# Top-k attention with a maxout layer on one core: small GpSimd steps moved to ScalarE, the k-th score chosen on VectorE, and the order planned anew

## The chip, the cores and the metric

The kernel runs on one core of one Trainium2 chip. The time is the device time of one execution in microseconds (us). The engines are TensorE (PE; its weight loads are listed apart as PEld), VectorE (DVE), ScalarE (ACT), GpSimd (POOL) and SyncE (SP), which here only issues DMAs. Each engine runs its own queue strictly in order and waits for the others by semaphores.

## The reference

Attention over 8 batches, 8 heads, 576 positions and 64 channels keeps for each query the 32 largest scores only; its output, 4608 tokens of 512 channels, goes through a layer that takes the maximum of three products, and an output product.

```python
scores = scale * np.matmul(q, k.transpose(0, 1, 3, 2))
kth = np.partition(scores, -top_k, axis=-1)[..., -top_k:-top_k + 1]
scores = np.where(scores >= kth, scores, -1000000000.0)
attn = np.exp(scores - np.max(scores, axis=-1, keepdims=True))
attn = attn / (np.sum(attn, axis=-1, keepdims=True) + 1e-09)
x = np.matmul(attn, v)            # heads side by side: 4608 x 512
h = np.maximum(np.maximum(x @ w1, x @ w2), x @ w3)
return h @ w_out
```

## The kernel before

The work on attention is cut into 80 units: 64 of four score tiles (nt = 4) and 16 of two (nt = 2), 288 tiles of 128 x 576 scores in all. Every unit passes these steps, named as in the code:

- `qk` (L514) multiplies on TensorE, `evac` (L523) copies the scores to SBUF on ScalarE.
- `sweep` (L532) takes the 8 largest of each stretch of 72 scores on VectorE. `negate` (L538) copies the 4 largest of each stretch with the sign turned, into the tile nA, on GpSimd. `pivot` (L546 to L563, VectorE) finds from both a first bound for the 32nd largest score; its fourth step writes z (L561).
- `sign` (L571, ScalarE) compares a tile with the bound and counts (cnt), `window` (L576, GpSimd) multiplies the scores with that sign, `below` (L580, VectorE) takes the 8 largest of the product. So nine candidates stand in Q.
- `place` (L588, L590, GpSimd) turns the count into a mask over the nine candidates (oh), `pick` (L596, L597, VectorE) multiplies it with Q and takes the maximum: the k-th score.
- `mask` (L620, VectorE) takes out what is smaller, `expo` (L629, ScalarE) makes exponentials and their sums.
- `denominator` (L637, GpSimd) adds 1e-9 to the sums (den), `inverse` (L644, VectorE) takes the reciprocal (rs), `widen` (L649, GpSimd) spreads it over 128 x 128 (rsw).
- `turn` (L675 to L680, TensorE) transposes exponentials and rsw, `turned` (L688, ScalarE) copies them out, `values` (L705, TensorE) multiplies with v, `scaled_x`, `high_x`, `low_x` (L722, L725, L729) scale the result and split it into two 16-bit parts.

The weights come in as 64-bit floats; `decode` (L238 to L240, three VectorE instructions) makes 32-bit ones of them in the first part of the run, and `cut` (L297 to L305) splits these. The feed-forward layers of a batch (`mlp`: products L761, maxima L768 and L770, split L773 and L776, output product L821) fill TensorE's gaps once the batch's attention is done; those of the last batch stand at the end.

The order of every engine's queue is made ahead of time, in Python, by `in_order` (L65 to L129). Every step is a `Piece` with an engine, an assumed cost in ns, the pieces that it needs and a rank: the place of its unit plus a number of the table OFFSETS (L38) for its kind. In a virtual time the planner takes for each engine the first piece by rank that could start within PATIENCE (L136) of the earliest; NEAR (L30) and LATE are assumed latencies between pieces, LEAD (L34) says how far ahead of the lowest rank a piece may be. TensorE takes a feed-forward piece where one can start earlier than attention's (L109 to L114). A piece marked `alone` starts, in this virtual time, only where GpSimd's last piece is about to end, and holds back GpSimd's next:

```python
        if x.alone:
            t = max(t, free["POOL"] + LOCK_A)
        elif x.engine == "POOL":
            t = max(t, shut[0] + LOCK_B)
```

In the kernel before, masks and the pivot's fourth step are marked so. On the chip only the order of each queue is left of the plan, and the semaphores.

Of the kernel before, what the change touches and what calls it, by code (L numbers as in the profile page):

```python
# [22 lines left out]
NW = 9  # L23
# [112 lines left out]
PATIENCE = {'PE': 45.0, 'DVE': 184.0, 'ACT': 29.0, 'POOL': 158.0, 'SP': 0.0}  # L136
# [1014 lines left out]
```

## Time and profile before

| | |
|---|---|
| three runs, us | 1317.75, 1319.06, 1319.50 (median 1319.06) |
| the profiled execution, us | 1317.94 |
| its span, us | 1315.6 |
| busy in the span: PE, DVE, ACT, POOL, us | 1179.5, 1188.1, 1069.0, 848.9 |
| granted TensorE clock, mean share of full speed | 0.98 |

The span runs from the first instruction of the profiled execution to its last; the execution's time has 2.3 us more around it. "Busy" is the time in which at least one instruction of an engine, or of a group of its instructions, was under way, waiting within the instruction included. A group is a line of the code, an engine, an operation and its tiles as out<-in, with the number of instructions behind the x.

### The profile page before, as it was taken

How to read it: one execution, taken by the hardware profiler on the slowest of the kernel's cores; microseconds unless marked ns; L12 is line 12 of the kernel's file. 1: busy time of each engine (PE TensorE's matmuls, PEld its weight loads, DVE VectorE, ACT ScalarE, POOL GpSimd, SP SyncE). 2: the span in 40 equal slices, each digit the busy share in tenths (PEclk: the TensorE clock that was granted, in tenths of full speed). 3: DMA queues.
4: the chain of work that ended last, by engine and by line, in shares of the span. 5: the costliest groups of instructions: out<-in, count | busy, mean ns of one | idle time of the engine just before them, and what ended most of it. 6: DMA issues, size and time to landing. Idle time of an engine off the chain costs nothing. (4 is left out here: it accounts for less than half of the span.)

```text
span 1315.6 us, 30962 instructions
## 1 busy us (share of the span) xinstructions
PE 1179.5 (90%) x9949; PEld 862.7 (66%) x9949; DVE 1188.1 (90%) x5656; ACT 1069.0 (81%) x2544; POOL 848.9 (65%) x1153
## 2 busy tenths in 40 slices
PE   4535897899799999999999999999999999999997
PEld 3323574666586676866676776767767676777775
DVE  7999998999999999999999999999999999997211
ACT  5778887999888989988898989899879998987221
POOL 4468588676677677776777586767676776755110
PEclk9999798999799999999999999999999999999999
DMA  6531110111111101111111011101111101000000
GB/s 184 175 105 36 49 37 25 39 37 37 38 27 36 35 22 52 29 44 25 31 46 27 27 38 44 37 27 28 38 35 29 45 19 35 10 17 1 17 17 28
DMA packets 107018, 53.59 MB, mean 41 GB/s; under 512 B 91744, under 2 KB 99936, under 8 KB 106848
## 3 DMA queue, kind: packets, MB, share of 16 engines
q1 hardware_dynamic: 106848, 51.54, 14.2%
q8 instruction: 80, 1.31, 0.4%
q14 instruction: 90, 0.74, 0.2%
HBM read 42.07 MB, written 9.44 MB: 39 GB/s over the span
## 5 line engine op out<-in xcount | busy, mean ns | idle before, releaser
L576 POOL TENSOR_TENSOR w<-ssb,w 128x576 f32<-128x576 f32 x288 | 423.8, 1479 | 67.9 <-ACT w L571 61.5
L761 PE MATMUL m<-xh,wall 128*128 128x256 f16 (+2 forms) x2448 | 437.0, 279 | 7.0 <-DVE h L770 5.7
L761 PEld LDWEIGHTS <-wall 128*128 128x128 f16 x3672 | 343.5, 98 | 87.5 <-issue 16.0
L761 PE MATMUL m<-xl,wall 128*128 128x256 f16 (+2 forms) x1224 | 335.3, 279 | 0.0
L532 DVE MAX8 L<-ssb 128x8 f32<-128x72 f32 x2304 | 331.3, 216 | 0.0
L620 DVE SCALAR_TENSOR_TENSOR ssb<-ssb,kth 128x576 f32<-128x576 f32 x288 | 262.1, 934 | 2.3
L629 ACT ACTIVATE pm<-ssb,nb 128x576 f32<-128x576 f32 x288 | 223.9, 779 | 43.7 <-DVE ssb L620 41.6
L571 ACT ACTIVATE w<-ssb,Q 128x576 f32<-128x576 f32 x288 | 224.0, 778 | 16.0 <-DVE Q L563 14.7
L688 ACT COPY pT<-tr 128x512 f32<-128x512 f32 (+1 forms) x432 | 216.4, 515 | 24.0 <-PE tr L677 12.2
L680 PE MATMUL tr<-ident,pm 128*128 128x128 f32 x1152 | 184.9, 288 | 48.8 <-ACT pm L629 15.0
L580 DVE MAX8 Q<-w 128x8 f32<-128x576 f32 x288 | 214.1, 748 | 6.4 <-POOL w L576 5.6
L514 PE MATMUL s<-kT,qT 64*128 64x288 f32 x1920 | 181.8, 326 | 20.7 <-ACT ssb L523 11.1
L680 PEld LDWEIGHTS tr<-ident,pm 128*128 128x128 f32 x1152 | 134.3, 145 | 99.4 <-ACT pm L629 31.0
L523 ACT COPY ssb<-s 128x576 f32<-128x576 f32 x288 | 182.1, 644 | 3.9 <-PE s L514 3.3
L514 PEld LDWEIGHTS s<-kT,qT 64*128 64x128 f32 x1920 | 143.1, 199 | 57.4 <-issue 21.3
L705 PE MATMUL tr<-pT,vt 128*64 128x256 f32 (+1 forms) x1920 | 180.3, 339 | 0.5 <-ACT pT L688 0.5
L770 DVE SCALAR_TENSOR_TENSOR h<-m,rises,h 128x256 f32<-128x256 f32 (+2 forms) x204 | 99.7, 489 | 75.5 <-PE m L761 72.5
L776 POOL TENSOR_TENSOR hl<-h,hh 128x256 f16<-128x256 f32 (+2 forms) x102 | 78.9, 774 | 112.3 <-ACT hh L773 111.1
L705 PEld LDWEIGHTS tr<-pT,vt 128*64 128x64 f32 x1920 | 109.4, 141 | 58.0 <-issue 13.3
L821 PE MATMUL m<-wall,hh 128*128 128x512 f16 x432 | 128.7, 379 | 2.6 <-POOL wall L305 1.7
L773 ACT CAST hh<-h 128x256 f16<-128x256 f32 (+2 forms) x102 | 42.5, 417 | 62.1 <-DVE h L770 61.7
L729 POOL TENSOR_TENSOR xl<-xs,xh 128x256 f16<-128x256 f32 (+1 forms) x80 | 56.9, 712 | 44.7 <-ACT xh L725 42.3
(110 smaller groups left out, 1540.8 us busy)
## 6 DMA issues: line engine op xcount, KB each, us to landing
wall<-in_moe_w_dram SPq DMA_DIRECT2D x12, 768.0 KB, 4.7
qt<-in_q_dram SPq DMA_DIRECT2D x68, 128.0 KB, 2.8
kt<-in_k_dram SPq DMA_DIRECT2D x68, 128.0 KB, 2.9
out_dram<-ob SPq DMA_DIRECT2D x32, 256.0 KB, 2.3
vt<-in_v_dram SPq DMA_DIRECT2D x32, 128.0 KB, 2.1
vt<-in_v_dram SPq DMA_DIRECT2D x32, 64.0 KB, 2.2
vt<-in_v_dram SPq DMA_DIRECT2D x96, 16.0 KB, 2.1
vt<-in_v_dram SPq DMA_DIRECT2D x32, 48.0 KB, 2.1
```

The lines of the kernel that those rows point to most:

```text
L514: nc.tensor.matmul(s[:, h, :HALF], qT[sl, qa, c0:c0 + P], kT[sl, ka, i * HALF:(i + 1) * HALF], start=(n_ == 0), stop=(n_ == len(runs) - 1))
L523: nc.scalar.copy(d["both", g][:, :, i * HALF:(i + 1) * HALF], d["s"].pop((g, i))[:, :, :HALF])
L532: nc.vector.max(d["L"][:, t, k, :], d["ssb"][t][:, k * GW:(k + 1) * GW])
L571: nc.scalar.activation(d["w"][t], d["ssb"][t], AF.Sign, bias=d["Q"][:, t, 0:1], scale=-1.0, accum_out=d["cnt"][:, t:t + 1])
L576: nc.gpsimd.tensor_tensor(d["w"][t], d["ssb"][t], d["w"][t], ALU.mult)
L580: nc.vector.max(d["Q"][:, t, 1:NW], d["w"].pop(t))
L620: nc.vector.scalar_tensor_tensor(ss, ss, d["kth"][:, t:t + 1], ss, ALU.is_lt, ALU.subtract, accum_out=d["lost"][:, t:t + 1])
L629: nc.scalar.activation(d["pm", t // 2][:, t % 2], d["ssb"][t], AF.Exp, bias=d["nb"][:, t:t + 1], scale=-1.0 / SHRINK, accum_out=d["sums"][ ...
L680: nc.tensor.transpose(pt[:, j * P:(j + 1) * P], pm[:, i, 64 * i + j * P:64 * i + (j + 1) * P], ident)
L688: nc.scalar.copy(pT[:, 512 * i:512 * i + m] if i < 2 else pT[:, 8 * P:10 * P], pt[:, :m])
L705: nc.tensor.matmul(to, vt[:, block if i < 4 else 8 + h, :], keys, start=(i == 0), stop=(i == 4))
L761: nc.tensor.matmul(box["ps", i][:, :c1 - c0], a, bb[:, kc, c0:c1], start=(kc == 0 and k == 0), stop=(kc == KC - 1 and k == 2))
```

## The change

Four things change.

1. `negate`, `denominator` and `widen` are issued on ScalarE instead of GpSimd.
2. `place` is gone. `pick` has three steps on VectorE: positions compared with the count (L591 of the new file), the product with Q (L594), the maximum (L596). The comparison gives the same 0 or 1 as the difference cut to between 0 and 1.
3. The first two steps of the choice, the weights' decoding and the review at a batch's end are marked `alone`, as masks were.
4. The planner's numbers: assumed costs of a dozen pieces, NEAR, AHEAD_OF_FILL, LEAD, PATIENCE, and all of the 84 OFFSETS. So the order of every queue is another one.

From the choice on, a line has a number lower by one in the new file (mask L619, exponentials L628, den L636, reciprocal L643, rsw L648, x L721, feed-forward product L760, maximum L769, output product L820).

```diff
-NEAR = 60.0
+NEAR = 110.0
...
-AHEAD_OF_FILL = 5
+AHEAD_OF_FILL = 3
...
-LEAD = 20.8
+LEAD = 43.3
...
-PATIENCE = {'PE': 45.0, 'DVE': 184.0, 'ACT': 29.0, 'POOL': 158.0, 'SP': 0.0}
+PATIENCE = {'PE': 2.0, 'DVE': 159.0, 'ACT': 47.0, 'POOL': 7.0, 'SP': 0.0}
...
-                    x = piece("DVE", 1870 if i < 3 else 2500, lambda j=j, j0=j0: decode(j, j0),
-                              [loads[j], *([decoded[j - 1]] if j else []), *([x] if j0 else [])], rank, [("ob", rel), ("ob", rel)])
+                    x = piece("DVE", 1600 if i < 3 else 1950, lambda j=j, j0=j0: decode(j, j0),
+                              [loads[j], *([decoded[j - 1]] if j else []), *([x] if j0 else [])], rank, [("ob", rel), ("ob", rel)], alone=True)
...
-        nc.gpsimd.tensor_scalar(nA[:, :d["nt"]], d["L"][:, :d["nt"], :, 0:4], -1.0, 1.0 / SHRINK, ALU.mult, ALU.mult)
+        nc.scalar.activation(nA[:, :d["nt"]], d["L"][:, :d["nt"], :, 0:4], AF.Copy, scale=-1.0 / SHRINK)
...
-        nc.gpsimd.tensor_tensor(oh[:, :nt], spots.unsqueeze(1).to_broadcast((P, nt, NW)),
-                                d["cnt"][:, :nt].unsqueeze(2).to_broadcast((P, nt, NW)), ALU.subtract)
-        nc.gpsimd.tensor_scalar(oh[:, :nt], oh[:, :nt], 1.0, 0.0, ALU.min, ALU.max)
...
+        if step == 0:
+            nc.vector.scalar_tensor_tensor(best[:, :nt], spots.unsqueeze(1).to_broadcast((P, nt, NW)), 1.0,
+                                           d["cnt"][:, :nt].unsqueeze(2).to_broadcast((P, nt, NW)), ALU.mult, ALU.is_gt)
+        elif step == 1:
+            nc.vector.tensor_tensor(best[:, :nt], best[:, :nt], d["Q"], ALU.mult)
+        else:
+            nc.vector.tensor_reduce(d["kth"], best[:, :nt], AX.X, ALU.max)
...
-        nc.gpsimd.tensor_scalar(d["den"][:, ts], d["sums"][:, ts], 1e-9, 1.0, ALU.add, ALU.mult)
+        nc.scalar.activation(d["den"][:, ts], d["sums"][:, ts], AF.Copy, bias=1e-9)
...
-        nc.gpsimd.tensor_scalar(rsw, d["rs"][:, 2 * g:2 * g + 2].unsqueeze(2).to_broadcast((P, 2, D)), 1.0, 1.0, ALU.mult, ALU.mult)
+        nc.scalar.copy(rsw, d["rs"][:, 2 * g:2 * g + 2].unsqueeze(2).to_broadcast((P, 2, D)))
...
-        p("i", "POOL", 380 + 44 * nt, lambda: place(n), needs=signs, takes=[("oh", held(n, "oh"))])
-        p("h", "DVE", 130 + 20 * nt, lambda: pick(n), needs=[d["i"], *ks])
-        held(n, "oh").append(d["h"])
+        for j in range(3):
+            p(("h", j), "DVE", 60 + 9 * nt, lambda j=j: pick(n, j), needs=[d["h", j - 1]] if j else [*signs, *ks],
+              takes=[] if j else [("oh", held(n, "oh"))], alone=j < 2)
+        held(n, "oh").append(d["h", 2])
...
-        x = piece("DVE", 1170, go, last, (rank, "R"), [("junk", rel)])
+        x = piece("DVE", 1016, go, last, (rank, "R"), [("junk", rel)], alone=True)
```

Three places of the orders. First VectorE, about the middle of the program, where the k-th scores of one unit are chosen and its first masks follow (oh: the mask over the candidates; kth: the chosen score). Before:

```order
L722 SCALAR_TENSOR_TENSOR xs<-tr,down_v,pT 128x128
L580 MAX Q<-w 128x8
L596 TENSOR_TENSOR oh<-oh,Q 128x36
L597 TENSOR_REDUCE kth<-oh 128x4
L532 MAX L<-ssb 128x8 x8
L620 SCALAR_TENSOR_TENSOR ssb,lost<-ssb,kth 128x576
```

Now:

```order
L580 MAX Q<-w 128x8
L591 SCALAR_TENSOR_TENSOR oh<-spots,cnt 128x36
L594 TENSOR_TENSOR oh<-oh,Q 128x36
L769 SCALAR_TENSOR_TENSOR h_9048<-m,rises,h_9018 128x320
L596 TENSOR_REDUCE kth<-oh 128x4
L619 SCALAR_TENSOR_TENSOR ssb,lost<-ssb,kth 128x576
```

The comparison is a VectorE step of its own ahead of the product; product, maximum and masks follow as before.

Second, the small steps that GpSimd loses. GpSimd before, in the same part of the program:

```order
L588 TENSOR_TENSOR oh<-spots,cnt 128x36
L590 TENSOR_SCALAR oh<-oh 128x36
L576 TENSOR_TENSOR w<-ssb,w 128x576
L776 TENSOR_TENSOR hl<-h_8631,hh 128x256
L637 TENSOR_SCALAR den<-sums 128x2
L649 TENSOR_SCALAR rsw<-rs 128x128
L474 TENSOR_TENSOR kT<-raws,kT 128x576
L637 TENSOR_SCALAR den<-sums 128x2
L649 TENSOR_SCALAR rsw<-rs 128x128
L538 TENSOR_SCALAR nA<-L 128x128
```

ScalarE now:

```order
L538 ACTIVATE nA<-L 128x128
L628 ACTIVATE pm,sums<-ssb,nb 128x576
L636 ACTIVATE den<-sums 128x2
L523 COPY ssb<-s 128x2x288
L724 CAST xh<-xs 128x2x64
L687 COPY pT<-tr 128x512
L648 COPY rsw<-rs 128x128
L687 COPY pT<-tr 128x512
L523 COPY ssb<-s 128x2x288
```

den, nA and rsw stand in ScalarE's queue, den behind the exponential that it needs, rsw after three other steps, with the evacuation of scores (L523) behind both; on GpSimd the windows, the splits and nothing small remain.

Third, the end of attention on VectorE, where the last result is scaled (L722) and the maxima of the remaining feed-forward layers follow (h). Before:

```order
L722 SCALAR_TENSOR_TENSOR xs<-tr,down_v,pT 128x128
L770 SCALAR_TENSOR_TENSOR h_20432<-m,rises,h_20392 128x320
L770 SCALAR_TENSOR_TENSOR h_20447<-m,rises,h_20432 128x320
L1080 TENSOR_REDUCE flag<-tr 1x1
L1082 CAST flag_i<-flag 1x1
L770 SCALAR_TENSOR_TENSOR h_20479<-m,rises,h_20464 128x320
L770 SCALAR_TENSOR_TENSOR h_20491<-m,rises,h_20479 128x320
L770 SCALAR_TENSOR_TENSOR h_20570<-m,rises,h_20555 128x256
```

Now:

```order
L721 SCALAR_TENSOR_TENSOR xs<-tr,down_v,pT 128x256
L721 SCALAR_TENSOR_TENSOR xs<-tr,down_v,pT 128x128
L1080 TENSOR_REDUCE flag<-tr 1x1
L1082 CAST flag_i<-flag 1x1
L769 SCALAR_TENSOR_TENSOR h_20490<-m,rises,h_20475 128x256
L769 SCALAR_TENSOR_TENSOR h_20505<-m,rises,h_20490 128x256
```

The four maxima of 320 columns that closed the batch before the last behind attention's end now stand ahead of it, and so do the products that they wait for.

## Rows read from the trace of the kernel before

**Rows 1.** Busy time by stage: us from:to, length, then busy time of each engine.

```profile
core 0: us, PE busy (x) PEld busy (x) DVE busy (x) ACT busy (x) POOL busy (x), PEclk, DMA share, GB/s
0.00:1213.00 1213.00, 1084.45 (x9055) 791.74 (x9056) 1169.23 (x5609) 1046.85 (x2492) 836.36 (x1131) 0.98 0.16 43
300.00:1213.00 913.00, 875.14 (x7553) 644.16 (x7550) 890.90 (x4427) 809.93 (x1935) 636.13 (x859) 0.99 0.12 32
1213.00:1316.00 103.00, 95.09 (x896) 70.94 (x894) 18.91 (x48) 22.19 (x52) 12.56 (x23) 0.99 0.06 20
1000.00:1100.00 100.00, 97.91 (x862) 71.23 (x861) 98.58 (x509) 91.66 (x222) 69.14 (x96) 1.00 0.10 25
```

**Rows 2.** The chain that ended last, end of attention: start us, length us, what.

```profile
1216.43 1.32 PE tr L705 x40
1217.75 2.55 PE m L761 x18
1220.41 4.89 PE m L761 x36
1225.30 7.77 PE m L821 x36
```

**Rows 3.** Groups of VectorE: count, busy us, mean ns, idle time before.

```profile
L620 DVE SCALAR_TENSOR_TENSOR ssb<-ssb,kth 128x576 f32<-128x576 f32 x288 | 262.1, 934 | 2.3
L596 DVE TENSOR_TENSOR oh<-oh,Q 128x36 f32<-128x36 f32 (+1 forms) x80 | 29.0, 362 | 2.5 <-POOL oh L590 0.3
L561 DVE SCALAR_TENSOR_TENSOR z<-n,b 128x32 f32<-128x32 f32 (+1 forms) x80 | 22.4, 280 | 1.2
L240 DVE SCALAR_TENSOR_TENSOR wall<-wall,ob 128x384 int32<-128x384 int32 (+1 forms) x27 | 23.2, 858 | 0.9
L239 DVE SCALAR_TENSOR_TENSOR ob<-wall,ob 128x384 int32<-128x384 int32 (+1 forms) x27 | 20.7, 768 | 0.9
```

**Rows 4.** The same by tile: shortest, median and longest in ns.

```profile
L620 DVE SCALAR_TENSOR_TENSOR ssb<-ssb,kth x288: 790/814/2027, 40.0 to 1209.2; 128x576 f32<-128x576 f32 x144
L596 DVE TENSOR_TENSOR oh<-oh,Q x80: 150/196/1311, 38.6 to 1208.0; 128x36 f32<-128x36 f32 x64, 128x18 f32<-128x18 f32 x16
L561 DVE SCALAR_TENSOR_TENSOR z<-n,b x80: 151/192/1385, 24.1 to 1195.8; 128x32 f32<-128x32 f32 x64, 128x16 f32<-128x16 f32 x16
L240 DVE SCALAR_TENSOR_TENSOR wall<-wall,ob x27: 557/559/1795, 12.6 to 166.5; 128x384 int32<-128x384 int32 x24, 128x512 int32<-128x512 int32 x3
L239 DVE SCALAR_TENSOR_TENSOR ob<-wall,ob x27: 557/565/1652, 11.0 to 165.8; 128x384 int32<-128x384 int32 x24, 128x512 int32<-128x512 int32 x3
```

**Rows 5.** Groups of GpSimd: the product, then the five that move.

```profile
L576 POOL TENSOR_TENSOR w<-ssb,w 128x576 f32<-128x576 f32 x288 | 423.8, 1479 | 67.9 <-ACT w L571 61.5 <-PE m L259 3.6
...
L649 POOL TENSOR_SCALAR rsw<-rs 128x128 f32<-128x128 f32 x144 | 52.4, 364 | 48.4 <-DVE rs L644 27.7 <-DVE oh L596 4.6 <-DVE z L561 4.5
...
L637 POOL TENSOR_SCALAR den<-sums 128x2 f32<-128x2 f32 x144 | 35.9, 249 | 74.7 <-ACT pm L629 66.0
L538 POOL TENSOR_SCALAR nA<-L 128x128 f32<-128x128 f32 (+1 forms) x80 | 27.7, 347 | 19.9 <-DVE L L532 17.9 <-DVE rs L644 0.5 <-DVE z L561 0.2
L588 POOL TENSOR_TENSOR oh<-spots,cnt 128x36 f32<-128x36 f32 (+1 forms) x80 | 22.5, 282 | 1.0
L590 POOL TENSOR_SCALAR oh<-oh 128x36 f32<-128x36 f32 (+1 forms) x80 | 17.7, 222 | 7.0
```

**Rows 6.** Groups of ScalarE, shapes kept apart: two small ones.

```profile
L725 ACT CAST xh<-xs 128x128 f16<-128x128 f32 x16 | 4.9, 303 | 5.4 <-DVE xs L722 5.4
...
L195 ACT COPY s<-tr 128x1 f32<-128x1 f32 x9 | 1.4, 157 | 0.0
```

**Rows 7.** Instructions in order of time, ScalarE near 701 us: start, length.

```profile
700.97 0.76 ACT L571 ACTIVATE w<-ssb,Q 128x576 f32<-128x576 f32 x1
...
701.63 0.19 ACT L571 ACTIVATION_READ_ACCUMULATOR w<-ssb,Q 128x1 f32 x1
701.72 0.76 ACT L571 ACTIVATE w<-ssb,Q 128x576 f32<-128x576 f32 x1
```

**Rows 8.** Who waited for whom, GpSimd: us in total, times, longest.

```profile
POOL rsw L649 <- DVE rs L644: 27.7, 36, 2.6
POOL nA L538 <- DVE L L532: 17.9, 17, 3.9
```

More of the change, by code (lines that the diff above doesn't have):

```diff
@@ L580, in below, with pick @@
         nc.vector.max(d["Q"][:, t, 1:NW], d["w"].pop(t))
-    def place(n):
+    def pick(n, step):
         d = st[n]
         nt = d["nt"]
-        oh = d["oh"] = sm.tile([P, 4, NW], F32, name="oh", bufs=2)
-        nc.gpsimd.tensor_tensor(oh[:, :nt], spots.unsqueeze(1).to_broadcast((P, nt, NW)),
-                                d["cnt"][:, :nt].unsqueeze(2).to_broadcast((P, nt, NW)), ALU.subtract)
-        nc.gpsimd.tensor_scalar(oh[:, :nt], oh[:, :nt], 1.0, 0.0, ALU.min, ALU.max)
-    def pick(n):
-        d = st[n]
-        oh = d["oh"][:, :d["nt"]]
-        nc.vector.tensor_tensor(oh, oh, d["Q"], ALU.mult)
-        nc.vector.tensor_reduce(d["kth"], oh, AX.X, ALU.max)
+        if step == 0:
+            d["oh"] = sm.tile([P, 4, NW], F32, name="oh", bufs=2)
+        best = d["oh"]
+        if step == 0:
+            nc.vector.scalar_tensor_tensor(best[:, :nt], spots.unsqueeze(1).to_broadcast((P, nt, NW)), 1.0,
[4 more added lines that the diff above has]
+            nc.vector.tensor_reduce(d["kth"], best[:, :nt], AX.X, ALU.max)
     def search(n):
@@ L790, in mlp @@
                     now = []
[L791 removed]
+                    y = add("DVE" if i else "ACT", 117 + 1.047 * w if i else 152 + 0.844 * w, lambda i=i, w=w, box=box: largest(i, w, box),
                             [x, *prev] if i else [x], [("h1", now)])
@@ L898, in attention @@
             rels = [[], []]
-            p(("q", g), "PE", 1680 if half else 890, lambda g=g: [qk(n, g, i) for i in range(2)], needs=needs, takes=[("s", rel) for rel in rels] + (takes if g == 0 else []),
+            p(("q", g), "PE", 1785 if half else 990, lambda g=g: [qk(n, g, i) for i in range(2)], needs=needs, takes=[("s", rel) for rel in rels] + (takes if g == 0 else []),
               mode="rows")
@@ L910, in attention @@
         swept = d["s", gs[-1], 1]
-        p("N", "POOL", 85 + 61 * nt, lambda: negate(n), needs=[swept], takes=[("nA", held(n, "nA"))])
+        p("N", "ACT", 104 + 27 * nt, lambda: negate(n), needs=[swept], takes=[("nA", held(n, "nA"))])
         p("p1", "DVE", 97 * nt, lambda: pivot(n, 1), needs=[swept] + ([of[n - 3]["p4"]] if n >= 3 else []))
@@ L939, in attention @@
             xs = [d["x", 2 * g], d["x", 2 * g + 1]]
-            p(("d", g), "POOL", 240, lambda g=g: denominator(n, g), needs=xs + ([d["d", 0]] if g else []), takes=[] if g else [("den", held(n, "den"))])
+            p(("d", g), "ACT", 95, lambda g=g: denominator(n, g), needs=xs + ([d["d", 0]] if g else []), takes=[] if g else [("den", held(n, "den"))])
             p(("r", g), "DVE", 72, lambda g=g: inverse(n, g), needs=[d["d", g]] + ([d["r", 0]] if g else []), takes=[] if g else [("rs", held(n, "rs"))])
-            p(("z", g), "POOL", 264, lambda g=g: widen(n, g), needs=[d["r", g]], takes=[("rsw", held(n, "rsw", g))])
+            p(("z", g), "ACT", 195, lambda g=g: widen(n, g), needs=[d["r", g]], takes=[("rsw", held(n, "rsw", g))])
             held(n, "den").append(d["r", g])
@@ L960, in attention @@
             takes.append(("x", x_done[b]))
-        p("v", "PE", 1300 if half else 8.6 * m + 60, lambda: values(n), needs=needs, takes=[("tr", rel)] + takes, mode="columns")
-        p("y", "DVE", 132 + 1.035 * m, lambda: scaled_x(n), needs=[d["v"]], takes=[("xs", held(n, "xs"))])
+        p("v", "PE", 1316 if half else 8.6 * m + 108, lambda: values(n), needs=needs, takes=[("tr", rel)] + takes, mode="columns")
+        p("y", "DVE", 119 + 1.035 * m, lambda: scaled_x(n), needs=[d["v"]], takes=[("xs", held(n, "xs"))])
         p("Y", "ACT", 91 + 0.86 * m, lambda: high_x(n), needs=[d["y"]])
```

11 lines of the change are left out of this document (5 added, 6 removed).

## The prediction

> **What bounds the kernel now.** I read the busy time by stage first. In the 1213 us until attention is over VectorE is busy for 1169.2 us and idle for 44; TensorE is busy for 1084.5, ScalarE for 1046.8 and GpSimd for 836.4 [rows 1]. So VectorE sets the length of that part (the body), though TensorE is not far behind: from 300 us on its share is 875.1 of 913, 95.9%, and the best 100 us of the whole run show 97.9% [rows 1]. Behind the body lies a tail of some 100 us in which VectorE is nearly empty and TensorE finishes the last batch's feed-forward layers [rows 1]. The chain of waits says the same at the end: after the last attention product come bare feed-forward products, one behind the other [rows 2]. The time is therefore the body, by VectorE's count, plus the tail, by TensorE's.
>
> Next, how much of VectorE's busy time is work. The mean of a mask is 934 ns, its median only 814 and its longest 2027 [rows 3, 4]; the product of the choice has 362 against 196, the pivot's step z 280 against 192, the two decoding steps with two inputs 858 against 559 and 768 against 565 [rows 3, 4]. These five take two inputs from SBUF, and in each the longest lies 1.1 to 1.2 us above the median. Mean less median, times the count: masks 120 ns x 288 = 34.6 us, choice 166 x 80 = 13.3, z 88 x 80 = 7.0, decoding 299 x 27 + 203 x 27 = 13.6. Together **68.5 us** of VectorE's "busy" is waiting. Now add what takes turns: those five groups are busy for 262.1 + 29.0 + 22.4 + 23.2 + 20.7 = 357.4 us [rows 3], GpSimd for 836.4 [rows 1]; the sum is 1193.8 of 1213. If they exclude each other, hardly a gap is left, and that is why they wait.
>
> **The change, part by part.** GpSimd loses five groups: 27.7 + 22.5 + 17.7 + 35.9 + 52.4 = 156.2 us [rows 5]. It was not the bound, so by itself that is worth nothing; it matters for the turns. With 156 us fewer, and 19 us more for the new step below, the turns fill about 1057 us, and the free time grows from 19 us (88, if the 68.5 us of waiting are not counted twice) to more than 150.
>
> ScalarE takes over 80 + 144 + 144 steps. The nearest rows are a 128x128 cast, 303 ns, for nA and rsw, and a copy of one column, 157 ns, for den [rows 6]: 224 x 0.303 + 144 x 0.157 = 90.5 us at most. Neighbours on ScalarE overlap: a sign that starts at 700.97 and lasts 0.76 is followed at 701.63, and the reading of its sum, 0.19 long, at 701.72 [rows 7], 0.1 us of overlap each. With that taken off, 224 x 0.203 + 144 x 0.057 = 53.7 us. I take 54, since ScalarE's queue is full enough for the overlap to be the rule. ScalarE then has 1046.8 + 53.7 = 1100.5 us in the body, 91.7% of 1200: what its best 100 us show now (91.66) [rows 1]. So I cost it at nothing, with VectorE as cover; without that cover it is a rival below.
>
> VectorE gets one more step for each of 80 units, the comparison of the positions with the count, because the two small GpSimd steps before the choice are now one VectorE step. Its nearest row is z, as small and also with two inputs: 192 ns at the median, 15.4 us, and 7.0 us of waiting at today's rate, none at best. The product and the maximum stay. The orders also show 3 or 4 more feed-forward maxima within the body: at most a mask's 0.814 us each, I take 2 us in all.
>
> How much of the waiting goes, no row of before shows. Bounds: none of it (the long GpSimd steps remain), or all 68.5 us. I take **one half**: the free time is multiplied several times over, which would remove more, but masks and z are already placed "between" GpSimd's steps in the order of before and still carry 41.6 of the 68.5 us, so a place in the order is not yet a place in time. Decoding, which has 13.6, had no such place and gets one. Body: -34.3 + 15.4 + 3.5 (half of the new step's 7.0) + 2 = **-13.4 us**.
>
> The tail: behind the last attention product TensorE's order has 54 feed-forward products of 320 columns and 21 of the output layer fewer (counted through to the end: 828 before, 753 now). 36 of the first kind take 4.89 us, 36 of the second 7.77 [rows 2]: 54 x 0.136 + 21 x 0.216 = **-11.8 us**. They go into the body, where TensorE must have room: of the 13.4 us some 6.8 (half of the decoding's) fall before 300 us, so the rest of the body has 906 us for 875.1 + 11.8 = 886.9 us of work: 97.8%, as much as its best stretch.
>
> Here a rule can be held against the row. The row: a mask can last 2027 ns where its median is 814 [rows 4], 1.2 us more, which is less than the 1479 ns of GpSimd's product [rows 5]. The Trainium skill, page "SBUF — State Buffer", section "Who interferes with whom", says that a VectorE instruction with two inputs in SBUF and a GpSimd one that reads SBUF cannot run at the same time, and that the later is blocked until the other has finished. This speaks against the new comparison, which becomes the sixth such instruction. By that rule, with which the trace's waits agree, it could cost up to a whole GpSimd product each time, 80 x 1.48 = 118 us. By the row of z, where most of the 80 found the way free, it is 7; I go by the row.
>
> Sum: 1317.94 us for the profiled execution, less 13.4 and 11.8, is 1292.7. The median of the runs, 1319.06, lies 1.1 above it: **1294 us**, 1.9% faster.
>
> **Rivals.**
> A, *ScalarE becomes the bound* (slower). Its three new steps wait for VectorE in a queue that never reorders. GpSimd waited 27.7 us for the reciprocal and 17.9 us for the sweep before the same steps [rows 8], where it delayed little; on ScalarE the evacuation of scores, signs and exponentials stand behind them, and VectorE waits for those. If ScalarE can't rise above the 88.7% that it holds from 300 us on (809.9 of 913 [rows 1]), the body needs 1100.5 / 0.887 = 1241 us, 28 more, less 11.8: 1335 us. It decides below a share of 89.9% (1100.5 / 1224.8). For it: the shares of three engines would all lie above 91%. Against: 91.66 has been seen. Chance 0.17, of it 0.02 near no change.
>
> B, *the change does not do what it says: VectorE waits as before*. What is long stays on GpSimd: 423.8 us in steps of 1479 ns, against 156.2 us in steps of 222 to 364 [rows 5]; a wait for a short step is short, and most of the waiting may be for long ones. With nothing saved the body grows by 15.4 + 7.0 + 2 = 24.4, less 11.8: 1332 us; with a fifth saved (13.7 and 1.4 of the new step's) it is 1317. The Trainium skill's page named above leans this way, since by it the wait lasts as long as the instruction that holds. Chance 0.16: 0.09 within 0.2%, 0.07 slower.
>
> C, *nearly all waiting goes, and TensorE is the bound*. VectorE would lose 68.5 - 17.4 = 51.1 us, but TensorE has 886.9 us to do after 300 us, so the body loses at most 913 - 886.9 = 26.1 there, and ahead of it the decoding's 13.6; with the tail 51.5: 1268 us. Against: no stretch shows TensorE without gaps. Chance 0.10.
>
> **How the numbers follow.** The forecast, waiting cut by a third to two thirds, has 0.57; its own range is 1281 to 1307. Faster: 0.57 + 0.10 = 0.67; within 0.2% (2.6 us, about what a measurement tells from no change): 0.11; slower: 0.15 + 0.07 = 0.22. The range, 1272 to 1328, reaches into C and over most of B and leaves out the upper half of A.
>
> **What would show it.** Right: masks at a mean near 870 ns, choice and z below 280, decoding steps below 700; GpSimd's busy time down by 156 us or more; VectorE's idle time in the body still some 45 us; ScalarE near 1100 us in the body; the last attention product near 1204 us and some 86 us of products behind the last of them instead of 98 (1217.75 to the end [rows 2]). Wrong: a mask's mean unchanged (B); ScalarE waiting for reciprocals and sweeps by tens of us, and VectorE's idle time grown with it (A); TensorE at 99% from 300 us on (C).

## The result: 3.0% faster, and the profile after

The median of four runs is 1278.54 us (1277.44 to 1279.52) against 1318.67 of four runs of the kernel before (1317.75 to 1319.50): a ratio of 0.9696, 95% interval 0.9679 to 0.9712, or 40.1 us less. The profiled execution took 1279.52 us. The head of its page:

```profile
span 1277.8 us, 30699 instructions
...
PE 1165.9 (91%) x9949; PEld 855.3 (67%) x9949; DVE 1157.3 (91%) x5736; ACT 1118.2 (88%) x2912; POOL 684.9 (54%) x625
```

Busy time by stage of the kernel after, in the columns of [rows 1]:

```profile
core 0: us, PE busy (x) PEld busy (x) DVE busy (x) ACT busy (x) POOL busy (x), PEclk, DMA share, GB/s
0.00:300.00 300.00, 213.13 (x1619) 150.93 (x1620) 280.37 (x1246) 255.42 (x650) 179.38 (x183) 0.86 0.26 76
300.00:1188.00 888.00, 870.40 (x7524) 641.90 (x7525) 860.55 (x4448) 843.15 (x2217) 494.73 (x423) 0.99 0.12 32
1188.00:1278.00 90.00, 82.38 (x809) 62.45 (x807) 16.41 (x43) 19.65 (x47) 10.76 (x20) 0.98 0.07 23
0.00:1188.00 1188.00, 1083.53 (x9142) 792.83 (x9143) 1140.92 (x5693) 1098.57 (x2866) 674.10 (x606) 0.96 0.16 43
500.00:600.00 100.00, 99.90 (x898) 77.10 (x897) 97.25 (x505) 94.69 (x245) 56.59 (x49) 1.00 0.14 36
```

Against [rows 1]: up to 1188 us (1213 before), 4 to 5 us short of attention's end, VectorE is busy for 1140.9 us instead of 1169.2, and idle for 47.1 instead of 43.8; ScalarE has 1098.6 instead of 1046.8, GpSimd 674.1 instead of 836.4. The end of the chain that ended last, as in [rows 2]:

```profile
1190.59 1.32 PE tr L704 x40
1191.90 3.34 PE m L820 x15
1195.25 1.31 PE m L760 x12
...
1196.66 22.27 PE m L760 x204
```

The last attention product ends at 1191.90 us where it was 1217.75: the body is 25.9 us shorter. From there to the end of the span are 85.9 us where 97.85 were: the tail is 11.95 us shorter. Together 37.8 us, the difference of the two spans.

The groups of VectorE that answer to [rows 3], with the comparison that is new and the decoding's first step:

```profile
L619 DVE SCALAR_TENSOR_TENSOR ssb<-ssb,kth 128x576 f32<-128x576 f32 x288 | 240.8, 864 | 2.3
L239 DVE SCALAR_TENSOR_TENSOR ob<-wall,ob 128x384 int32<-128x384 int32 (+1 forms) x27 | 20.2, 747 | 0.9
L240 DVE SCALAR_TENSOR_TENSOR wall<-wall,ob 128x384 int32<-128x384 int32 (+1 forms) x27 | 19.6, 725 | 0.9
L561 DVE SCALAR_TENSOR_TENSOR z<-n,b 128x32 f32<-128x32 f32 (+1 forms) x80 | 19.4, 242 | 1.3
L591 DVE SCALAR_TENSOR_TENSOR oh<-spots,cnt 128x36 f32<-128x36 f32 (+1 forms) x80 | 17.9, 224 | 0.0
L594 DVE TENSOR_TENSOR oh<-oh,Q 128x36 f32<-128x36 f32 (+1 forms) x80 | 16.5, 206 | 2.4
L238 DVE TENSOR_SCALAR ob<-wall 128x384 int32<-128x384 int32 (+1 forms) x27 | 12.8, 473 | 8.2 <-DMA wall<-in_moe_w_dram 8.2
```

The same by tile, shortest, median and longest in ns, as in [rows 4]:

```profile
L619 DVE SCALAR_TENSOR_TENSOR ssb<-ssb,kth x288: 793/816/2075, 63.5 to 1182.8; 128x576 f32<-128x576 f32 x144
L594 DVE TENSOR_TENSOR oh<-oh,Q x80: 152/196/543, 62.2 to 1181.2; 128x36 f32<-128x36 f32 x64, 128x18 f32<-128x18 f32 x16
L591 DVE SCALAR_TENSOR_TENSOR oh<-spots,cnt x80: 151/178/1298, 60.2 to 1180.7; 128x36 f32<-128x36 f32 x64, 128x18 f32<-128x18 f32 x16
L561 DVE SCALAR_TENSOR_TENSOR z<-n,b x80: 151/191/1199, 24.0 to 1171.3; 128x32 f32<-128x32 f32 x64, 128x16 f32<-128x16 f32 x16
```

Medians have not moved (a mask 816 ns, 814 before), means have. The work is the same, the waiting is less. Mean less median times the count, as in the prediction: masks (864 - 816) x 288 = 13.8 us, product 0.8, z 4.1, decoding 5.1 + 4.5 (medians 559 and 559): 28.3 us where 68.5 were. The longest mask is still 2075 ns: a single wait is as long as before, there are fewer of them.

The GpSimd product, and ScalarE's new steps:

```profile
L576 POOL TENSOR_TENSOR w<-ssb,w 128x576 f32<-128x576 f32 x288 | 413.6, 1454 | 135.2 <-ACT w L571 134.3
...
L648 ACT COPY rsw<-rs 128x128 f32<-128x128 f32 x144 | 43.9, 307 | 3.1 <-DVE rs L643 2.6
...
L636 ACT ACTIVATE den<-sums 128x2 f32<-128x2 f32 x144 | 30.7, 215 | 0.6
L538 ACT ACTIVATE nA<-L 128x128 f32<-128x128 f32 (+1 forms) x80 | 24.6, 307 | 4.1 <-DVE L L532 3.9
```

ScalarE waits 2.6 us for reciprocals and 3.9 for sweeps, where GpSimd waited 27.7 and 17.9 [rows 8].

**Who holds VectorE.** One reading of the traces settles most of what follows, so it stands ahead of the runs. For each instruction of the masks, the choice, the pivot's fourth step and the decoding that lasts over 100 ns longer than its group's median, take the GpSimd instruction that is under way when it starts. In the kernel before these are some 125 waits of 79 us in all behind GpSimd's long steps (the window's product, the splits of x and h, the transposed q and k, the weights), and 2 or 3 waits of under 0.5 us behind the small ones (nA, den, rsw, oh). After: some 70 waits, 38 us, all behind long ones. The limit of 100 ns hides next to nothing: with the review, 66 of the 546 instructions of before start in a small step, and all that they last beyond their medians comes to 0.6 us. In a long step 176 of the 546 start before, and 123 of 626 after: long steps are met less often. Two examples, start and length. Before, near 434 us, VectorE and GpSimd rows of the instructions in order of time:

```profile
433.45 0.22 POOL L590 TENSOR_SCALAR oh<-oh 128x36 f32<-128x36 f32 x1
433.62 1.42 POOL L576 TENSOR_TENSOR w<-ssb,w 128x576 f32<-128x576 f32 x1
433.79 1.86 DVE L620 SCALAR_TENSOR_TENSOR ssb<-ssb,kth 128x576 f32<-128x576 f32 x1
435.00 1.31 POOL L776 TENSOR_TENSOR hl<-h,hh 128x320 f16<-128x320 f32 x1
435.59 0.08 DVE L620 DVE_READ_ACCUMULATOR ssb<-ssb,kth 128x1 f32 x1
```

The mask starts 0.17 us into the product, lasts 1.86 us where the median is 814 ns, and ends at 435.65, 0.61 us after the product (435.04). The split behind the product starts within the mask and is long in turn: 1.31 us. After, near 470 us:

```profile
469.68 0.87 POOL L775 TENSOR_TENSOR hl<-h,hh 128x320 f16<-128x320 f32 x1 [2.41 <-ACT hh L772]
...
469.82 0.08 DVE L619 DVE_READ_ACCUMULATOR ssb<-ssb,kth 128x1 f32 x1
469.82 1.34 DVE L619 SCALAR_TENSOR_TENSOR ssb<-ssb,kth 128x576 f32<-128x576 f32 x1
```

Here the holder is a split of the same 128x320, 0.87 us when it comes first; the mask takes 1.34 and ends, again, 0.61 us after it. That is no accident: of the masks over 1 us that start within such a holder, all 46 of before and all 18 of after end 611 to 620 ns after their holder's end.

### The profile page after: what moved, and what is told of

It reads as the page before. It is cut to its first block, busy times and chain, and to the rows that moved or that the text cites. A ratio compares the mean times of both kernels' runs of the same rounds, so it can differ in the third digit from the quotient of the medians.

```text
span 1277.8 us, 30699 instructions
## 1 busy us (share of the span) xinstructions
PE 1165.9 (91%) x9949; PEld 855.3 (67%) x9949; DVE 1157.3 (91%) x5736; ACT 1118.2 (88%) x2912; POOL 684.9 (54%) x625
## 3 DMA queue, kind: packets, MB, share of 16 engines
q8 instruction: 80, 1.31, 0.4%
## 4 chain that ended last, share of the span: by engine, by line
PE 33%; DVE 26%; ACT 20%; POOL 4%; issue 2%; SPq 0%; DMA 0%; ACTq 0%; DVEq 0%; POOLq 0%
PE m L760 16%; DVE L L532 6%; DVE ssb L619 6%; DVE Q L580 4%; ACT w L571 4%; PE m L820 4%; ACT pm L628 4%; PE tr L704 4%; ACT pT L687 4%; PE tr L679 4%; POOL w L576 3%; PE s L514 3%; ACT ssb L523 3%; DVE h L769 2%; DVE nR L556 1%
## 5 line engine op out<-in xcount | busy, mean ns | idle before, releaser
L576 POOL TENSOR_TENSOR w<-ssb,w 128x576 f32<-128x576 f32 x288 | 413.6, 1454 | 135.2 <-ACT w L571 134.3
L760 PE MATMUL m<-xh,wall 128*128 128x256 f16 (+2 forms) x2448 | 436.9, 279 | 1.3 <-DVE h L769 0.6
L760 PEld LDWEIGHTS <-wall 128*128 128x128 f16 x3672 | 343.8, 98 | 79.7 <-issue 7.4
L760 PE MATMUL m<-xl,wall 128*128 128x256 f16 (+2 forms) x1224 | 335.2, 279 | 0.0
L532 DVE MAX8 L<-ssb 128x8 f32<-128x72 f32 x2304 | 329.7, 219 | 2.2 <-ACT ssb L523 2.2
L619 DVE SCALAR_TENSOR_TENSOR ssb<-ssb,kth 128x576 f32<-128x576 f32 x288 | 240.8, 864 | 2.3
L628 ACT ACTIVATE pm<-ssb,nb 128x576 f32<-128x576 f32 x288 | 225.5, 785 | 18.5 <-DVE ssb L619 18.3
L523 ACT COPY ssb<-s 128x576 f32<-128x576 f32 x288 | 185.0, 646 | 4.2 <-PE s L514 3.8
L679 PEld LDWEIGHTS tr<-ident,pm 128*128 128x128 f32 x1152 | 130.8, 143 | 80.2 <-ACT pm L628 27.3
L769 DVE SCALAR_TENSOR_TENSOR h<-m,rises,h 128x256 f32<-128x256 f32 (+2 forms) x204 | 100.4, 492 | 60.1 <-PE m L760 55.9
L820 PE MATMUL m<-wall,hh 128*128 128x512 f16 x432 | 128.9, 379 | 3.6 <-POOL wall L305 1.9
L728 POOL TENSOR_TENSOR xl<-xs,xh 128x256 f16<-128x256 f32 (+1 forms) x80 | 52.4, 655 | 126.6 <-ACT xh L724 126.6
L474 POOL TENSOR_TENSOR kT<-raws,kT 128x576 fp32r<-128x576 f32 x34 | 49.7, 1462 | 86.2 <-ACT kT L470 83.8
```

Source lines behind the costliest of these rows:

```text
L523: nc.scalar.copy(d["both", g][:, :, i * HALF:(i + 1) * HALF], d["s"].pop((g, i))[:, :, :HALF])
L532: nc.vector.max(d["L"][:, t, k, :], d["ssb"][t][:, k * GW:(k + 1) * GW])
L576: nc.gpsimd.tensor_tensor(d["w"][t], d["ssb"][t], d["w"][t], ALU.mult)
L619: nc.vector.scalar_tensor_tensor(ss, ss, d["kth"][:, t:t + 1], ss, ALU.is_lt, ALU.subtract, accum_out=d["lost"][:, t:t + 1])
L628: nc.scalar.activation(d["pm", t // 2][:, t % 2], d["ssb"][t], AF.Exp, bias=d["nb"][:, t:t + 1], scale=-1.0 / SHRINK, accum_out=d["sums"][ ...
L679: nc.tensor.transpose(pt[:, j * P:(j + 1) * P], pm[:, i, 64 * i + j * P:64 * i + (j + 1) * P], ident)
```

## The experiments

Each kernel ran beside runs of the kernel before (medians 1318.2, 1318.7 and 1318.96 us for the three groups below). In the expectations T is the theory of the prediction: GpSimd's small steps took turns, and with them gone VectorE waits less. N is a rival: the planner's new numbers, and so the order, bring the gain. F was formed later: only long steps hold VectorE, and what counts is how well the order fits the code that it is planned for.

All times are in us. "Waiting" is mean less median times the count, line by line of the code, summed over masks, product, comparison, z, all decoding steps (the first one and the three of 512 columns included) and the review. Taken tile by tile it comes out up to 5 us higher or lower, so differences of a few us in it say little. "Body" runs to the start of the last attention product, "tail" from that product's end to the last computing instruction. Idle time and GpSimd's busy time are those of the body.

| kernel | median | ratio to before, 95% | body | tail | waiting | VectorE idle | GpSimd busy |
|---|---|---|---|---|---|---|---|
| before | 1318.7 | 1 | 1217.5 | 91.7 | 75.9 | 48 | 837 |
| after | 1278.5 | 0.9696 (0.9679 to 0.9712) | 1191.7 | 79.8 | 39.4 | 51 | 675 |
| e1 numbers alone | 1337.7 | 1.0142 (1.0125 to 1.0159) | 1218.5 | 111.2 | 67.0 | 67 | 818 |
| e2 code alone | 1325.3 | 1.0048 (1.0031 to 1.0064) | 1230.8 | 87.6 | 53.3 | 71 | 675 |
| e3 small steps on GpSimd, after's order | 1326.4 | 1.0055 (1.0037 to 1.0073) | 1239.5 | 80.1 | 56.7 | 80 | 780 |
| e4 the same, planned anew | 1298.3 | 0.9842 (0.9826 to 0.9859) | 1202.6 | 90.8 | 44.2 | 60 | 786 |
| e5 no new `alone` | 1330.7 | 1.0088 (1.0061 to 1.0115) | 1245.1 | 77.9 | 58.6 | 79 | 674 |
| e9 choice as before | 1333.9 | 1.0109 (1.0090 to 1.0129) | 1237.5 | 89.2 | 59.5 | 86 | 712 |
| e6 736 extra GpSimd steps that read | 1299.2 | 0.9854 (0.9833 to 0.9875) | 1210.8 | 79.8 | 48.9 | 59 | 870 |
| e7 736 extra GpSimd steps that only write | 1290.8 | 0.9789 (0.9770 to 0.9809) | 1202.2 | 79.8 | 47.7 | 53 | 753 |
| e8 288 extra ScalarE copies | 1304.5 | 0.9892 (0.9871 to 0.9912) | 1216.8 | 79.8 | 34.6 | 76 | 673 |
| e10 before, three steps on ScalarE | 1345.0 | 1.0197 (1.0179 to 1.0216) | 1242.2 | 91.7 | 77.2 | 66 | 728 |
| e11 after, offsets nudged | 1302.9 | 0.9873 (0.9853 to 0.9894) | 1209.7 | 84.3 | 46.8 | 61 | 679 |
| e12 before, offsets nudged | 1404.2 | 1.0640 (1.0620 to 1.0660) | 1340.9 | 57.6 | 92.8 | 133 | 828 |

### The numbers, the code, the small steps

**e1, the numbers alone.** Issue and choice as before; the planner's numbers and assumed costs are the change's, no step is newly marked `alone`. The choice's one step takes the first of its three new offsets, `place` keeps its old one. Against the kernel before:

```diff
-NEAR = 60.0
+NEAR = 110.0
...
-AHEAD_OF_FILL = 5
+AHEAD_OF_FILL = 3
...
-LEAD = 20.8
+LEAD = 43.3
...
```

> The code of before with the planner's new numbers and assumed costs; no step changes its engine, none is newly marked alone. Theory T (VectorE's waiting for turns with GpSimd is what went, and it went because GpSimd has fewer steps): GpSimd stays busy for some 840 us, a mask keeps a mean of 900 ns or more, the five groups' waiting stays at 55 us or more, and the tail after the last attention product is longer than before (the order has 144 more products of 320 columns there): 1310 to 1340 us. Theory N (the new order alone made the gain): 1295 us or less, a mask's mean near 860 ns.

Measured: 1337.7 us, 1.4% slower than before. The body is as long as before, the tail 20 us longer. N is out in its plain form: the numbers by themselves bring no gain, as T had it.

**e2, the code alone.** The kernel after with the planner's numbers of before; the three steps of the choice all get the offset that the one step had:

```diff
-NEAR = 110.0
+NEAR = 60.0
...
-'h0': 2.46, 'h1': -2.33, 'h2': 1.34
+'h0': -4.05, 'h1': -4.05, 'h2': -4.05
...
```

> The changed code and its assumed costs with the planner's old numbers (the three steps of the choice all get the old number of the choice). T: the waiting goes as in the change, a mask's mean is 850 to 890 ns, VectorE's busy time falls by 20 us or more, and the tail is 4 us shorter than before by its order: 1285 to 1302 us. N: within 10 us of before, 1308 to 1328 us.

Measured: 1325.3 us, 0.5% slower than before. Waiting does fall, from 75.9 to 53.3, and VectorE's busy time in the body by 10 us, but it is idle for 71 us instead of 48, and the body grows by 13. The time is far above T's range and in N's (1308 to 1328), though e1 had put N out: neither theory covers both runs. Neither half gains alone (+19.5 and +7.1 us against the runs of before beside them), both together gain 40.

**e3, the small steps issued on GpSimd in after's order.** Every queue otherwise as after:

```diff
-        nc.scalar.activation(nA[:, :d["nt"]], d["L"][:, :d["nt"], :, 0:4], AF.Copy, scale=-1.0 / SHRINK)
+        nc.gpsimd.tensor_scalar(nA[:, :d["nt"]], d["L"][:, :d["nt"], :, 0:4], -1.0, 1.0 / SHRINK, ALU.mult, ALU.mult)
...
-        nc.scalar.activation(d["den"][:, ts], d["sums"][:, ts], AF.Copy, bias=1e-9)
+        nc.gpsimd.tensor_scalar(d["den"][:, ts], d["sums"][:, ts], 1e-9, 1.0, ALU.add, ALU.mult)
...
-        nc.scalar.copy(rsw, d["rs"][:, 2 * g:2 * g + 2].unsqueeze(2).to_broadcast((P, 2, D)))
+        nc.gpsimd.tensor_scalar(rsw, d["rs"][:, 2 * g:2 * g + 2].unsqueeze(2).to_broadcast((P, 2, D)), 1.0, 1.0, ALU.mult, ALU.mult)
```

> The changed kernel with its order of steps untouched, but the three small steps (nA, den, rsw) issued on GpSimd again. T: GpSimd is busy for some 110 us more, a mask's mean rises to 900 ns or more, VectorE's busy time by 15 to 35 us: 1295 to 1315 us. Rival (the gain came from the order, or from GpSimd's small steps as suppliers that came late): the waiting stays near 32 us and the time within 6 us of the change, 1273 to 1285 us.

Measured: 1326.4 us; the body is 48 us longer than after, 17 of it waiting. The largest new wait is a plain one, as the list of waits (us in total, times, longest) shows:

```profile
DVE rs L643 <- POOL den L636: 27.9, 39, 1.6
```

den stands in GpSimd's queue behind a long step, and VectorE's reciprocal waits for it; after has 2.4 us there. The time lies above both ranges; the waiting and a mask's mean (905 ns) come as T had it, so this run by itself would have spoken for T.

**e4, the same, but planned as GpSimd's steps**, so that the order is another:

```diff
-        p("N", "ACT", 104 + 27 * nt, lambda: negate(n), needs=[swept], takes=[("nA", held(n, "nA"))])
+        p("N", "POOL", 85 + 61 * nt, lambda: negate(n), needs=[swept], takes=[("nA", held(n, "nA"))])
...
```

> As the last, but the planner knows that the three small steps are GpSimd's, with their old assumed costs, so the order is another one; the choice stays on VectorE. T: a plan that knows cannot give the turns back: a mask's mean 890 ns or more, the tail 11 us longer than the change's by its order: 1298 to 1318 us. Rival: planning finds places for them, the waiting stays near 32 us, and only the tail is lost: 1286 to 1294 us.

Measured: 1298.3 us, 1.6% faster than before, with all three steps on GpSimd. GpSimd is busy for 786 us, 111 more than after, yet VectorE waits 44.2 us, 4.8 more. Half the loss against after, 11 of 20 us, is the tail. The time lies at the lower edge of T's range, but T's sign does not come: a mask's mean is 867 ns, where T named 890 or more. So moving the three steps is not what removes the waiting.

### A part undone, a load added

**e5, no new `alone`.** The choice, the decoding and the review lose the mark:

```diff
-              takes=[] if j else [("oh", held(n, "oh"))], alone=j < 2)
+              takes=[] if j else [("oh", held(n, "oh"))])
...
-        x = piece("DVE", 1016, go, last, (rank, "R"), [("junk", rel)], alone=True)
+        x = piece("DVE", 1016, go, last, (rank, "R"), [("junk", rel)])
```

> The changed kernel without the new marks: decoding, the first two steps of the choice and the review are planned as any other step (masks and z keep their mark); the order is planned anew. Theory M (the marks are what cut the waiting of these steps): the product of the choice and the comparison wait for 12 us or more in sum as before the change instead of 4.5, all waiting 48 us or more instead of 39, 1288 us or more though its order has 2 us less in the tail. Theory P (the waiting fell because the plan's time fits the chip's better and GpSimd has fewer steps; the marks add little): waiting within 5 us of the change's, 1274 to 1286 us.

Measured: 1330.7 us, 0.9% slower than before. M's signs come, P's do not. The groups of the comparison, the product and the review:

```profile
L591 DVE SCALAR_TENSOR_TENSOR oh<-spots,cnt 128x36 f32<-128x36 f32 (+1 forms) x80 | 27.7, 346 | 0.0
L594 DVE TENSOR_TENSOR oh<-oh,Q 128x36 f32<-128x36 f32 (+1 forms) x80 | 22.9, 287 | 2.6
...
L656 DVE TENSOR_TENSOR junk<-Q,kth 128x324 f32<-128x324 f32 x8 | 8.8, 1096 | 0.0
```

Unmarked, the choice's two steps wait 13.3 + 7.3 us; marked, 3.7 + 0.8. So within these numbers the marks on the choice go with 16 us less of its waiting, and those on the review with some 4. For the decoding they do nothing: unmarked it waits 12.2 us, marked 16.3, before 19.6. The other half of the loss is idle time, 28 us more than after: the table of offsets is that of the marked kernel.

**e9, the choice as before**: `place` on GpSimd and the one-step `pick`, planned anew, the rest as after.

```diff
+        nc.gpsimd.tensor_tensor(oh[:, :nt], spots.unsqueeze(1).to_broadcast((P, nt, NW)),
+                                d["cnt"][:, :nt].unsqueeze(2).to_broadcast((P, nt, NW)), ALU.subtract)
+        nc.gpsimd.tensor_scalar(oh[:, :nt], oh[:, :nt], 1.0, 0.0, ALU.min, ALU.max)
...
-        for j in range(3):
-            p(("h", j), "DVE", 60 + 9 * nt, lambda j=j: pick(n, j), needs=[d["h", j - 1]] if j else [*signs, *ks],
...
+        p("i", "POOL", 380 + 44 * nt, lambda: place(n), needs=signs, takes=[("oh", held(n, "oh"))])
+        p("h", "DVE", 130 + 20 * nt, lambda: pick(n), needs=[d["i"], *ks])
...
```

> The changed kernel with the choice as before: two small steps on GpSimd make the mask over the candidates, product and maximum follow on VectorE; nA, den and rsw stay on ScalarE, the order is planned anew. If the choice's move saved the waiting of its product: that waits for 8 us or more again, VectorE loses the 17.9 us of the comparison, GpSimd gains 40 us; with a tail that is 9 us longer by its order 1283 to 1297 us. If the choice's place was worth nothing by itself: the tail alone, 1287 us or below with the product's waiting under 3 us.

Measured: 1333.9 us, above both ranges. GpSimd has only 37 us more than after, but waiting is 20 us higher (masks 24.3, product 7.8), idle time 35 us, the tail 9. Read as above, all but 0.4 us of some 58 stand behind long steps, none behind the two small ones that are back; as with e5 the part and the misfit of the numbers come in one.

**e6, 736 more GpSimd steps in after's order**, two behind each of the moved ones, without use for the result:

```diff
+        nc.gpsimd.tensor_scalar(spare, ident[:, :32], 1.0, 1.0, ALU.mult, ALU.mult)
+        nc.gpsimd.tensor_scalar(spare, ident[:, :32], 1.0, 1.0, ALU.mult, ALU.mult)
...
```

> The changed kernel in its own order, with two more small GpSimd steps (128x32, read and written in SBUF, used by nobody) at each of the 368 places where a small step was taken from it: some 155 us more on GpSimd, which nobody waits for directly. Theory T (GpSimd's small steps cost VectorE its turns): waiting rises by 15 us or more to 55 us, 1294 to 1312 us. Theory P: small steps hardly make VectorE wait, they only delay GpSimd's own long ones, and GpSimd idles for 517 us of the body: waiting below 47 us, 1278 to 1290 us.

Measured: 1299.2 us. One of the six new groups, and the wait that grew:

```profile
L655 POOL TENSOR_SCALAR spare<-ident 128x32 f32<-128x32 f32 x144 | 42.1, 293 | 11.9
```

```profile
DVE Q L583 <- POOL w L579: 18.3, 35, 1.9
```

GpSimd works 195 us more in the body than in after, more than the change had taken from it. If load took turns, all the gain in waiting should be gone. It grows by 9.5 us, of 36.5, which lies between what T named (15 or more) and what P did (below 47 in all); the time is T's, not P's. Read as above, some 86 waits of 46 us stand behind long steps and 6 at most, under 1 us in all, behind small ones, the new ones included. The other half of the loss is plain lateness: VectorE waits 18.3 us for windows, 8.3 in after.

**e8, 288 more copies on ScalarE in after's order**:

```diff
+        nc.scalar.copy(spare, ident[:, :32])
+        nc.scalar.copy(spare, ident[:, :32])
```

> The changed kernel in its own order, with two more small ScalarE copies (128x32, used by nobody) behind each of the 144 rsw steps: some 35 us more of ScalarE's time. If ScalarE has become a bound beside VectorE (it is busy for 94 to 97% from 300 us on): 15 to 40 us more, 1293 to 1318 us. If VectorE still covers it, as the prediction had it: at most 6 us more, below 1285 us.

Measured: 1304.5 us. The list of waits of VectorE:

```profile
DVE Q L581 <- POOL w L577: 21.6, 45, 1.8
DVE rs L644 <- ACT den L637: 8.8, 26, 0.8
```

42 us more on ScalarE make the body 25 us longer, all of it idle time on VectorE (76 instead of 51), though waiting even falls. So this load is not covered by VectorE: in after's order ScalarE, busy for 92% of the body without the copies, is a bound beside it.

### The order against the load

**e10, the kernel before with `negate`, `denominator` and `widen` on ScalarE**, its own order kept: the three issue lines of e3 the other way round, in the old file.

```diff
-        nc.gpsimd.tensor_scalar(d["den"][:, ts], d["sums"][:, ts], 1e-9, 1.0, ALU.add, ALU.mult)
+        nc.scalar.activation(d["den"][:, ts], d["sums"][:, ts], AF.Copy, bias=1e-9)
...
```

> The kernel before in its own order, with the three small steps (nA, den, rsw) issued on ScalarE at the places that the planner gave them on GpSimd. Theory T (fewer GpSimd steps free the turns): VectorE's waiting falls from 76 us to 60 or less, and more than pays for ScalarE's load: 1290 to 1312 us. Theory F (a step counts by how it fits into the queues' order; taking load from GpSimd by itself is worth little): the waiting falls by less than 12 us or VectorE idles for what it saves, and ScalarE's 54 us delay the rest: 1314 to 1345 us.

Measured: 1345.0 us, 2.0% slower. The masks' group and the wait that is new:

```profile
L620 DVE SCALAR_TENSOR_TENSOR ssb<-ssb,kth 128x576 f32<-128x576 f32 x288 | 266.4, 950 | 1.8
```

```profile
DVE rs L644 <- ACT den L637: 15.0, 31, 1.5
```

This is the plainest test of T. GpSimd loses 109 us, and VectorE waits 77.2 us where it waited 75.9; a mask's mean goes from 934 [rows 3] to 950 ns. And the body grows by 25 us: where nothing else changes, the move costs, 14 of it by reciprocals that now wait for den on ScalarE (15.0 us, where 1.0 went to den on GpSimd), the kind of wait that rival A described, one step further on. The time lies at the upper edge of F's range.

**e11 and e12, every offset moved by 0.3**, up and down in turn, in after and in before. Nothing but the order changes:

```diff
-OFFSETS = {'C0': -8.46, 'C1': -18.47, 'C2': 3.93, 'C3': 15.97,
+OFFSETS = {'C0': -8.16, 'C1': -18.77, 'C2': 4.23, 'C3': 15.67,
...
```

> The changed kernel with each of the 84 numbers of the table moved by 0.3, up and down in turn (units stand 2 apart for four tiles): the same code and load, another order that no one has fitted to it. Its tail is 4.5 us longer by the order. If the table is fitted to this order to the last decimals (F): waiting 45 to 60 us and VectorE idle for 70 us or more in the body, 1300 to 1335 us. If load and marks make the gain (T): within 10 us, 1278 to 1292 us.

> The kernel before with each number of its table moved by 0.3 in the same way. F: before was fitted too, so it loses as much as the change does under the same treatment, 1330 to 1370 us. If the gain is that only the new table is well fitted: before loses little, 1315 to 1328 us, while the changed kernel loses 20 us or more.

Measured: 1302.9 us for after (24 more) and 1404.2 for before (85 more). Waiting rises by 7.4 and 16.9 us, idle time by 10 and 85. F's range takes in the first, though its idle time is 61 us where 70 or more was named; the second lies above both ranges: F had both kernels lose alike, and before loses 85 us, after 24. In e12 VectorE waits 39.5 us for windows (5.6 before), 16.8 for scores and 14.4 for den. So the loads of the engines, unchanged here, say little about the time: one small step away from the table costs that much beside the 40 us that the change wins. It is one pattern of steps in each kernel.

**e7, 736 GpSimd steps that only write**, at the places of e6:

```diff
+        nc.gpsimd.memset(spare, 0.0)
+        nc.gpsimd.memset(spare, 0.0)
...
```

> As the run with two extra small GpSimd steps at 368 places, in the changed kernel's order, but each only writes a constant (128x32) and reads nothing. If a GpSimd step makes VectorE's two-input steps wait only while it reads: waiting stays at 36 to 43 us (48.9 with the reading steps), z and the comparison at 8 us in sum instead of 15. If any GpSimd step does: 46 us or more. The time follows GpSimd's delay of its own long steps in both: 1283 to 1296 us.

Measured: 1290.8 us, 126 ns each. Waiting is 47.7 us, nearly that of e6 with its steps of some 280 ns, and again all but 0.5 us of it lies behind long steps. By the ranges this is "any GpSimd step", but in both the extra steps act by shifting the long ones in time. Whether a writing step by itself can hold VectorE is not told by this: neither kind held it for much more than 1 us in all.

No kernel here beats the change.

## Why the prediction was right, and where its reason was not

**Time and sign: right, too small.** Forecast 25 us, measured 38.4 for the profiled execution and 40.1 for the medians; both lie in the range. Nearly all that is missing is the body: it is 25.9 us shorter where 13.4 was forecast, and attention ends at 1191.9 us where near 1204 was named. Of the difference 5.9 us are waiting and 6.0 steps that were not priced, both below.

**The tail: right.** -11.8 us from the count of products behind the last attention product, -11.95 measured.

**ScalarE's load: right.** 1100.5 us forecast for the body, 1098.6 measured. Costing it at nothing held in this order: rival A's wait did not come. It does not hold as a rule: e8 and e10, which load ScalarE as well, lengthen the body by 25 us each.

**The comparison: right.** 18.9 us forecast with its waiting, 17.9 measured, 3.7 of it waiting.

**The waiting: size roughly right, reason wrong.** One half, 34.3 us, was to go; 40.2 went. Masks came to 864 ns (named: near 870), product and z to 206 and 242 (under 280); the decoding stayed at 747 and 725, where under 700 was named. That one half came near is luck: no row gave the share, and the reason for it does not hold. The step that failed is the one on turns: that GpSimd's 156 us of small steps fill the turns, so that without them the free time is multiplied. It added up busy times as if any GpSimd instruction could hold VectorE. The attribution shows 79 us of waiting behind long steps and under 0.5 behind small ones; e10 takes 109 us of small steps away and waiting stays; e4 keeps them and waiting still falls from 75.9 to 44.2; e6 puts 195 us back and a quarter of it returns. Rival B had the premise right (a wait for a short step is short, what is long stays on GpSimd) and drew the wrong end from it: long steps can stay and still hold VectorE less often, some 70 times instead of 125, if the queues are ordered so. By the Trainium skill, page "SBUF — State Buffer", section "Who interferes with whom", the later of two such instructions is blocked until the other has finished. The rows agree but for some 170 ns: the wait is set by what the holder has left to run, and a held mask ends 611 to 620 ns after it, where the shortest mask takes 790. How often that happens the page does not say, and that is what changed.

**Not priced: 6.0 us.** VectorE's busy time in the body fell by 28.3 us. The waiting of the five groups makes -40.2, the comparison +17.9, and the rest is -6.0: the decoding's first step, with one input, from 16.5 to 12.8 us; the decoding of 512 columns, from 9.2 to 8.0; the review, from 5.9 to 4.8. Their groups of before, and the review's of after:

```profile
L238 DVE TENSOR_SCALAR ob<-wall 128x384 int32<-128x384 int32 (+1 forms) x27 | 16.5, 611 | 8.2 <-DMA wall<-in_moe_w_dram 8.2
L657 DVE TENSOR_TENSOR junk<-Q,kth 128x324 f32<-128x324 f32 x8 | 5.9, 741 | 0.0
```

```profile
L656 DVE TENSOR_TENSOR junk<-Q,kth 128x324 f32<-128x324 f32 x8 | 4.8, 594 | 0.0
```

All three had waited too, and were left out because the rows were chosen by "two inputs" and by size. The four moved maxima are there (164 in 82.5 us before, 168 in 85.4 after: 2.9 us, 2 forecast); small differences in the other groups, the sweep's 331.3 to 329.7 us among them, take as much away.

**TensorE's room: too strict.** The check took 97.9% as the best that TensorE had shown. That was misread: from 1200 to 1300 us, mostly tail, the kernel before shows 99.4%. After the change TensorE holds 98.0% from 300 us on and 99.9% in single stretches, and the same products took 1165.9 us of busy time instead of 1179.5. So rival C's floor was no floor.

**What stays open.** How the 40 us divide among the parts. The numbers alone lose 20 us and the code alone 7, so the parts don't add; each undone part (e4, e5, e9) got an order from the changed kernel's numbers, and its loss is part and misfit in one. No run gives the code of before a table made anew for it, so it is not shown that a gain of this size needs the new code. What is shown is that small steps hold VectorE for next to nothing, that taking three of the five kinds away in the order of before frees no waiting, that the marks on the choice cut its own waiting within one set of numbers, and that with equal loads the time moves by 24 and 85 us with the order.

## What to carry to other kernels

Before a wait is credited to an engine's load, list the waits one by one with the instruction that held them: here some 125 waits behind long steps explained nearly all, and 156 us of small steps next to nothing. Test a moved step with the queues otherwise as they are; if that costs (25 us here), the gain is not in the move by itself, and parts undone one at a time need not add up to it (e1 and e2 lose 20 and 7 us, both together gain 40). Where two engines hold each other, price every instruction that shows a mean above its median, also those with one input.

## What the runs showed of the hardware that was not expected

- A mask that has waited ends 611 to 620 ns after the instruction that held it, in 64 of 64 cases (masks over 1 us), though the shortest mask takes 790 ns: some 170 ns of it pass while it waits.
- An instruction with one input can wait as well: the decoding's first step (128x384, int32) has a mean of 473 ns after and lasts between 334 and 936 ns. The four of 384 columns that last over 650 ns end 215 to 219 ns after the GpSimd step in which they started.
- Small ScalarE steps that overlap their neighbours still cost: 288 copies of about 223 ns each, 42 us of busy time, lengthened the body by 25 us.
- In the first 100 us of the profiled executions TensorE was granted 0.73 of its full clock after and 1.00 before, with 40.95 us busy instead of 47.35, so a part of that stretch ran at 1.2 GHz. VectorE's busy time there is the same (87.25 and 87.67 us). That the change brings this about is not shown: executions of the kernel before have a mean clock from 0.946 to 0.980 over the whole run, and their times lie within 0.5% of each other.
